# A fused chunk attention and two-layer network: the first layer in seven products for blocks 5 to 18, with sums in PSUM, and a new order

## The chip, the cores and the metric

The kernel runs on one core of a Trainium2 chip. The metric is the device time of one execution in microseconds (us); the median of three runs before the change is 275.13 us (274.96 to 275.59).

## The reference

Attention runs inside chunks of 64 tokens, for 8 batches of 576 tokens and 8 heads of 64 columns; its output, as 4608 rows of 512 columns, goes through two matrices with a leaky ReLU between them.

```python
scores = scale * np.matmul(q_c, k_c.transpose(0, 1, 2, 4, 3))   # chunks of 64 x 64
scores = scores - np.max(scores, axis=-1, keepdims=True)
attn = np.exp(scores)
attn = attn / (np.sum(attn, axis=-1, keepdims=True) + 1e-09)
out = np.matmul(attn, v_c)
...
x = np.ascontiguousarray(attn_out.transpose(0, 2, 1, 3)).reshape(B * S, H * D)
h = x @ w_in                     # 4608 x 512 by 512 x 2048
g = np.maximum(0.01 * h, h)
return (g @ w_out)               # 2048 x 512
```

## The kernel before

The tokens are worked through in 36 groups `u` of 128 rows (two chunks of all heads) for the attention, and in 19 blocks `j` for the two layers: two blocks of 128 rows, then seventeen of 256. The order of all instructions is written out by hand in one string, `ORDER`; each word is a step with its numbers, and every engine works through its own instructions strictly in the order in which the words stand.

The steps of the attention for a group are: `g` loads q and k (DMA from POOL's queue), `tq`/`tk` transpose them on PE and `q`/`k` copy them (groups 0 to 13), or `tdq`/`tdk` transpose them by a DMA from SP's queue and `cq` copies q (later groups); `s` scores (PE), `m` their maximum and `b` the subtraction (DVE), `x` the exponential (ACT), `z` sum and reciprocal (DVE), `n` the product with it (DVE, from group 10 on POOL); `e` and `c` transpose the result on PE for the first groups, `d` by DMA for the others; `v` multiplies with V (PE) and `a` copies the result to `xT` (ACT), the input of the first layer. `i` are idle products of PE that only read a constant tile; `iN` is N units of 128 columns, issued three at a time. `y` and `w` clear tiles.

The first layer of blocks 0 to 8 is plain: steps `M` (in blocks 0 to 2 partly named `A`) of 16 products of 128 columns or 8 of 256 columns each (line 319), eight per block of 256 rows, and one activation `G` (line 333, leaky ReLU from PSUM to `gT`) for each. For blocks 9 to 18 it is computed with seven products of half size in place of eight (Strassen's scheme in Winograd's form): `WS` builds four differences of w_in once, `xs` four sums of x per block (POOL or DVE, line 387), `V j.s.n` is product n for half s of the hidden columns, eight matmuls of 128 columns (line 416). Products 1, 6, 7 and 4 pile up in one bank of PSUM; after 1, 6 and 7 `lx` copies the running sum to SBUF (ACT, line 447). Products 2, 5 and 3 have other banks, and `la` adds them to those copies (DVE, line 453). `lp`, and `lx` after product 4, apply the leaky ReLU (line 435).

The second layer uses the same scheme for blocks 2 to 18: `W` builds four differences of w_out, `sum` four sums of `gT` (line 203), `R j.n` is product n, eight matmuls of 256 columns (line 227), `comb` copies (ACT, line 260) or adds (DVE, lines 264 and 281) the results and issues the store from SP's queue. Blocks 0 and 1 use plain products `B` (line 462). The last product, `R18.4`, is cut in two halves so that the first half's add and store run beside the second (line 244).

PSUM has eight banks. Before the change four of them have fixed users (`qp`, `kp`, `Sp`, `ox`) which some of the products share, and four go by the string `BANKS`.

Of the kernel before, what the change touches and what calls it, by code (L numbers as in the profile page):

```python
# [16 lines left out]
def kernel(  # L17
# [36 lines left out]

# [3 lines left out]


# [5 lines left out]
    xT = sbp.tile([128, NT, RING], FP16, name="xT")  # L65
    qk: dict[int, tuple[bass.AP, bass.AP]] = {}

    made: set[tuple] = set()

    def need(*what):  # L70
        assert what in made, what

    def load_qk(u):

        both = []
        for name, src in (("q_in", q), ("k_in", k)):
# [18 lines left out]
    def load_v_heads(b, m, h0, h1):  # L95
        if b >= NVB:
            need("batch", b - NVB)
        nc.gpsimd.dma_start(  # L98
            out=VB[b % NVB][m * CH:(m + 1) * CH, h0:h1, :, m * CH:(m + 1) * CH].rearrange("p h c d -> p (h c) d"),
            in_=v[b, m * H // 2 + h0:m * H // 2 + h1].rearrange("h (c j) d -> j (h c) d", j=CH),  # L100
        )

    def load_v(b):
        for m in range(2):
            load_v_heads(b, m, 0, H // 2)

    def load_w_in(f0, f1):
        for m in range(2):
            nc.gpsimd.dma_start(
                out=w_inT[m * CH:(m + 1) * CH, :, f0:f1],  # L110
                in_=moe_w_in[m * d_model // 2:(m + 1) * d_model // 2, f0:f1].rearrange("(t d) f -> d t f", d=D),
            )
# [51 lines left out]
    SG: dict[tuple[int, int], bass.AP] = {}
    bank: dict[tuple[int, str], bass.AP] = {}
    kept: dict[tuple[int, str], bass.AP] = {}
    opened: set[tuple[int, str]] = set()

    def weight_sum(n):
        b11, b12 = w_outT[:, :HF, :HM], w_outT[:, :HF, HM:]  # L170
        b21, b22 = w_outT[:, HF:, :HM], w_outT[:, HF:, HM:]
        x, y = {1: (b12, b11), 2: (b22, TW.get(1)), 3: (b22, b12), 4: (b21, TW.get(2))}[n]
        TW[n] = sbp.tile([128, HF, HM], FP16, name=f"TW{n}")
        nc.vector.tensor_tensor(out=TW[n], in0=x, in1=y, op=ALU.subtract)

    def rows(j):

        nh = BLOCKS[j] // 2
        halves_of = slice(0, nh), slice(nh, 2 * nh)
        return halves_of[::-1] if j in EARLY else halves_of  # L180

    def token_sums(j, n):
        if (j, n) in SG:
            return
        if j in EARLY:
            for a, p in {
                1: [(a, 1) for a in range(4)], 2: [(0, 2), (1, 2)], 3: [(0, 1), (1, 1), (0, 2), (1, 2)], 4: [(2, 2), (3, 2)],
            }[n]:
                need("act", j, a, p)
        if n in (2, 4):  # L190
            token_sums(j, n // 2)
        nh = BLOCKS[j] // 2
        one, two = rows(j)
        a11, a12 = gT[j][:, :HF, one], gT[j][:, HF:, one]
        a21, a22 = gT[j][:, :HF, two], gT[j][:, HF:, two]
        SG[j, n] = sbp.tile([128, HF, nh], FP16, name="SG", tag="gS", bufs=4, padded_shape=[128, HF, 128])
        x, y, op = {
            1: (a21, a22, ALU.add),
            2: (SG.get((j, 1)), a11, ALU.subtract),
            3: (a11, a21, ALU.subtract),  # L200
            4: (a12, SG.get((j, 2)), ALU.subtract),
        }[n]
        (nc.gpsimd if (j, n) in SG_POOL else nc.vector).tensor_tensor(out=SG[j, n], in0=x, in1=y, op=op)  # L203

    def product(j, n, i):
        one, two = rows(j)
        g, w = gT[j], w_outT
        where, left, right = {
            1: ("X", g[:, :HF, one], w[:, :HF, :HM]),
            2: ("W", g[:, HF:, one], w[:, HF:, :HM]),  # L210
            3: ("Z", SG.get((j, 4)), w[:, HF:, HM:]),
            4: ("X", g[:, HF:, two], TW.get(4)),
            5: ("Z", SG.get((j, 1)), TW.get(1)),
            6: ("X", SG.get((j, 2)), TW.get(2)),
            7: ("X", SG.get((j, 3)), TW.get(3)),
        }[n]
        if where != "X" and j in ONE:
            where = n
        if (j, where) not in bank:
            tag = None if j in EARLY else {"X": "qp", "Z": None if j in ZMM else "kp"}.get(where)  # L220
            bank[j, where] = psp.tile([128, 2, HM], FP32, name=f"pr{where}", tag=tag or mm(), bufs=1)
        to = bank[j, where]
        if j == LAST and n == 4:
            last_product(left, right)
            return
        for f in range(HF):
            nc.tensor.matmul(  # L227
                out=to[:, i, :],
                lhsT=left[:, f, i * 128:(i + 1) * 128],
                rhs=right[:, f, :],  # L230
                start=(j, where) not in opened,
# [119 lines left out]
    def w_in_sum(n):  # L351
        if len(WS) >= n:
            return
# [519 lines left out]
```

## Time and profile before

| | |
|---|---|
| time, median of three runs | 275.13 us |
| span of the profiled execution (its time beside the span isn't given) | 273.3 us |
| busy PE / DVE / ACT / POOL | 265.9 / 219.9 / 208.8 / 165.3 us |
| products of the plain first layer, line 319 | 768 |
| products of the first layer in seven, line 416 | 1120 |
| products of the second layer in seven, line 227 | 944 |
| granted clock of PE | 1.00 |

The span runs from the first to the last instruction. A row of a timeline gives start and length in us, engine, line, operation, the tile written and the tiles read. A group of products ends in the records some time after its last product could be followed by another, so the spacing of two starts is shorter than a group's length; the chain of waits shows the spacing.

### The profile page before, as it was taken

What the parts mean: (1) busy time and instruction counts of PE and PEld (TensorE: products, weight loads), DVE (VectorE), ACT (ScalarE), POOL (GpSimd) and SP (SyncE); (2) the same over time, 40 slices, a digit from 0 to 9 for tenths busy, and PEclk for the clock granted to TensorE, in tenths of its full rate; (3) what the DMA queues carried; (4) which work ended last, traced back from release to release, by engine and by line L of the source; (5) the groups of instructions that cost most, each with busy time, mean ns of one, the idle gap of its engine ahead of it and who ended that gap; (6) DMA issues with size and microseconds to landing.
All of it is one profiled execution on the core that took longest, in us unless ns stands there. A gap on an engine that the chain in (4) does not pass through costs nothing.

```text
span 273.3 us, 9009 instructions
## 1 busy us (share of the span) xinstructions
PE 265.9 (97%) x3705; PEld 242.4 (89%) x3705; DVE 219.9 (80%) x427; ACT 208.8 (76%) x410; POOL 165.3 (60%) x190
## 2 busy tenths in 40 slices
PE   7889999999999999999999999999999999999994
PEld 3579958999999899998989999999999998999994
DVE  7786869999997668798677987977899879488783
ACT  6667635665779688666999989899999998857560
POOL 8848546783175448649689799689895636012100
PEclk9999999999999999999999999999999999999999
DMA  9999999999999999999999999799999503131113
GB/s 147 155 188 191 206 178 156 176 117 130 210 138 169 171 140 119 195 219 168 164 189 153 203 160 124 139 134 180 95 147 158 134 2 101 22 98 40 41 41 115
DMA packets 159241, 38.34 MB, mean 140 GB/s; under 512 B 150240, under 2 KB 154720, under 8 KB 159200
## 3 DMA queue, kind: packets, MB, share of 16 engines
q0 software_dynamic: 111392, 18.10, 98.3%
q1 hardware_dynamic: 46768, 19.41, 38.7%
q8 instruction: 29, 0.48, 0.7%
q10 hardware_dynamic: 1040, 0.26, 0.4%
q14 instruction: 12, 0.10, 0.2%
HBM read 36.70 MB, written 9.44 MB: 169 GB/s over the span
## 4 chain that ended last, share of the span: by engine, by line
PE 86%; DVE 5%; ACT 3%; POOL 3%; issue 2%; POOLq 0%; DVEq 0%; ACTq 0%
PE hT L319 20%; PE prX L227 20%; PE xbank L416 11%; PE xpr L416 9%; PE prZ L227 6%; PE pr L227 6%; PE prW L227 3%; PE Sp L584 3%; PE xp L656 3%; PE oP L462 3%; ACT QZ L539 1%; ACT gT L435 1%; PE kp L512 1%; PE qp L512 1%; POOL SG L203 1%
## 5 line engine op out<-in xcount | busy, mean ns | idle before, releaser
L319 PE MATMUL hT<-xT,w_inT 128*128 128x128 f16 (+1 forms) x768 | 62.4, 237 | 0.0
L319 PEld LDWEIGHTS <-w_inT 128*128 128x128 f16 x768 | 53.6, 98 | 2.8
L227 PEld LDWEIGHTS <-SG 128*128 128x128 f16 x544 | 51.0, 98 | 5.4
L620 POOL TENSOR_TENSOR en<-ex,zi 128x512 f16<-128x512 f16 x26 | 28.2, 1085 | 40.1 <-DVE zi L614 19.8
L453 DVE TENSOR_TENSOR xkeep<-xpr,xkeep 128x512 f32<-128x512 f32 x60 | 39.6, 681 | 13.7 <-ACT xkeep L447 9.6
L333 ACT ACTIVATE gT<-hT 128x512 f16<-128x512 f32 x64 | 36.6, 595 | 9.0 <-PE hT L319 8.9
L227 PEld LDWEIGHTS <-gT 128*128 128x128 f16 x400 | 37.3, 98 | 4.3 <-ACT gT L435 0.4
L447 ACT ACTIVATE xkeep<-xbank 128x512 f32<-128x512 f32 x60 | 34.6, 593 | 7.4 <-PE xbank L416 7.0
L416 PEld LDWEIGHTS <-WS 128*128 128x128 f16 x640 | 38.0, 98 | 0.5
L91 POOL DMA_DIRECT2D q_in<-in_q_dram x39 | 33.4, 861 | 7.0 <-DMA w_outT<-in_moe_w_out_dram 3.0
L91 POOL DMA_DIRECT2D k_in<-in_k_dram x39 | 32.6, 838 | 7.8 <-DMA VB<-in_v_dram 3.3
L227 PE MATMUL prX<-TW,SG 128*128 128x256 f16 x272 | 35.3, 273 | 0.0
L435 ACT ACTIVATE gT<-xkeep 128x512 f16<-128x512 f32 x56 | 33.4, 631 | 2.1 <-DVE xkeep L453 1.8
L260 ACT ACTIVATE keep<-prX 128x256 f32<-128x256 f32 x51 | 19.6, 384 | 16.9 <-PE prX L227 16.5
L416 PEld LDWEIGHTS <-w_inT 128*128 128x128 f16 x480 | 29.0, 98 | 0.9 <-issue 0.4
L203 DVE TENSOR_TENSOR SG<-gT 128x1024 f16<-128x1024 f16 x34 | 25.2, 740 | 4.7 <-ACT gT L333 2.9
L610 DVE TENSOR_REDUCE z<-ex 128x8 f32<-128x512 f16 x36 | 24.4, 679 | 4.9 <-ACT ex L604 4.7
L593 DVE TENSOR_REDUCE mx<-Sp 128x8 f32<-128x512 f32 x36 | 24.4, 677 | 4.5 <-PE Sp L584 4.5
L573 ACT ACTIVATE QZ<-QT 64x512 f16<-64x512 f16 x44 | 27.3, 627 | 0.9 <-PE Sp L584 0.3
L677 ACT ACTIVATE xT<-xp 128x512 f16<-128x512 f32 x36 | 21.5, 596 | 6.0 <-PE xp L656 5.8
L387 POOL TENSOR_TENSOR xs<-xT 128x256 f16<-128x256 f16 x18 | 12.5, 701 | 20.7 <-ACT xT L677 20.7
L98 POOL DMA_DIRECT2D VB<-in_v_dram x24 | 23.4, 987 | 0.0
(92 smaller groups left out, 486.0 us busy)
## 6 DMA issues: line engine op xcount, KB each, us to landing
out_dram<-osb SPq DMA_DIRECT2D x35, 256.0 KB, 4.1
q_in<-in_q_dram POOLq DMA_DIRECT2D x31, 128.0 KB, 5.9
k_in<-in_k_dram POOLq DMA_DIRECT2D x31, 128.0 KB, 6.7
VB<-in_v_dram POOLq DMA_DIRECT2D x8, 288.0 KB, 9.1
VB<-in_v_dram POOLq DMA_DIRECT2D x16, 144.0 KB, 5.3
w_inT<-in_moe_w_in_dram POOLq DMA_DIRECT2D x8, 256.0 KB, 7.2
w_outT<-in_moe_w_out_dram POOLq DMA_DIRECT2D x4, 512.0 KB, 11.6
q_in<-in_q_dram POOLq DMA_DIRECT2D x8, 64.0 KB, 6.3
```

What stands on the lines that cost most here:

```text
L91: nc.gpsimd.dma_start(out=to, in_=rows)
L203: (nc.gpsimd if (j, n) in SG_POOL else nc.vector).tensor_tensor(out=SG[j, n], in0=x, in1=y, op=op)
L227: nc.tensor.matmul(out=to[:, i, :], lhsT=left[:, f, i * 128:(i + 1) * 128], rhs=right[:, f, :], start=(j, where) not in opened, stop=(f == ...
L319: nc.tensor.matmul(out=hT[:, i, :], lhsT=w_inT[:, t, fc * 128:(fc + 1) * 128], rhs=xT[:, t, r0:r0 + tb], start=(t == 0), stop=(t == NT - 1),)
L333: nc.scalar.activation(out=gT[j][:, nf * a:nf * a + nf, c0:c0 + tb], in_=HT.pop((j, a, p)), func=AFT.Prelu, bias=0.0, scale=1.0, alpha=0.01,)
L416: nc.tensor.matmul(out=to[:, i, :], lhsT=left[:, t, i * 128:(i + 1) * 128], rhs=right[:, t], start=(n in (1, 2, 5) and t == 0 and i == 0), ...
L435: nc.scalar.activation(out=gT[j][:, f0:f0 + 4, hi * 128:hi * 128 + 128], in_=of, func=AFT.Prelu, bias=0.0, scale=1.0, alpha=0.01)
L447: nc.scalar.activation(out=XK[j, s, n], in_=XB[j, s], func=AFT.Copy, bias=0.0, scale=1.0)
L453: nc.vector.tensor_tensor(out=to, in0=of, in1=to, op=ALU.add)
L573: nc.scalar.activation(out=to, in_=QT[u][part], func=AFT.Copy, bias=0.0, scale=1.0)
L593: nc.vector.tensor_reduce(out=MX[u], in_=SP[u], axis=AXL.X, op=ALU.max)
L620: (nc.gpsimd if u >= UP else nc.vector).tensor_tensor(out=E[u], in0=ex, in1=ZI.pop(u).unsqueeze(2).to_broadcast((128, 8, CH)), op=ALU.mult)
```

## The change

The first layer of blocks 5 to 8 goes over to seven products; blocks 0 to 4 stay plain. In all fourteen blocks with seven products the sums are formed in another way: after product 1 a copy `ls` puts it in a second bank of PSUM (`seed`), on which product 2 is accumulated; product 5 is copied to SBUF (`lf`); `la` adds that copy to the sum of products 1 and 6, back into the bank of product 5, on which product 3 is then accumulated, and to the sum of products 1, 6 and 7; product 4 is accumulated in the first bank. Four activations `lp` read the three banks and the one tile in SBUF.

All steps stand in a new order, with `z` cut in three, `W` and `WS` in two, and the stores as steps `st` of their own. A word that ends in `'` runs on the other engine of its kind: copies on DVE in place of ACT, sums and `n` on POOL in place of DVE, the leaky ReLU on DVE, the small addition in `z` on ACT. The second string, `BANKS`, now names the bank of each of PSUM's tiles and the buffer of each tile in SBUF; some tiles get more buffers (`KT` 4 for 3, `ex` 4 for 2, `en` 4 for 3, `et` 5 for 4, sums of `gT` 5 for 4).

```diff
...
+    def copy(other, to, of):
+        if other:
+            nc.vector.tensor_copy(out=to, in_=of)
         else:
+            nc.scalar.activation(out=to, in_=of, func=AFT.Copy, bias=0.0, scale=1.0)
...
+    def leaky(other, to, of):
+        if other:
+            nc.vector.scalar_tensor_tensor(out=to, in0=of, scalar=0.01, in1=of, op0=ALU.mult, op1=ALU.max)
+        else:
+            nc.scalar.activation(out=to, in_=of, func=AFT.Prelu, bias=0.0, scale=1.0, alpha=0.01)
...
+    def wide(j, s, n):
...
+        if n == 1:
+            XB[j, s] = ps([128, 4, 128], "xbank")
+        elif n == 5:
+            XZ[j, s] = ps([128, 4, 128], "xz")
+        to = {2: XW, 3: XZ, 5: XZ}.get(n, XB)[j, s]
+        for i in range(4):
+            for t in range(2):
+                nc.tensor.matmul(
+                    out=to[:, i, :],
+                    lhsT=left[:, t, i * 128:(i + 1) * 128],
+                    rhs=right[:, t],
+                    start=(n in (1, 5) and t == 0 and i == 0),
+                    stop=(t == 1),
+                    skip_group_check=True,
+                )
+
+    def wide_seed(j, s, other=0):
+        XW[j, s] = ps([128, 4, 128], "seed")
+        copy(other, XW[j, s], XB[j, s])
+
+    def wide_five(j, s, other=0):
+        X5[j, s] = sb([128, 4, 128], FP32, "x5", "xkeep", 6)
+        copy(other, X5[j, s], XZ[j, s])
+
+    def wide_add(j, s, n):
+        to = XZ[j, s] if n == 3 else X5[j, s]
+        nc.vector.tensor_tensor(out=to, in0=XB[j, s], in1=X5[j, s], op=ALU.add)
+
+    def wide_leaky(j, s, n, other=0):
+        second, hi = {2: (0, 0), 4: (0, 1), 3: (1, 0), 5: (1, 1)}[n]
+        of = {2: XW, 4: XB, 3: XZ, 5: X5}[n][j, s]
+        f0 = 8 * s + 4 * second
+        leaky(other, hidden(j)[:, f0:f0 + 4, hi * 128:hi * 128 + 128], of)
...
     ORDER = (
-        "i33 y4 y2 I y0 y6 y1 tq0 q0.0 q0.1 w3 tk0 i5 k0 i6 s0 tq1 i4 m0 b0 q1.1.1 i13 tk1 q1.0.1 x0 k1 tq2 i8 s1 tk2 "
-        "z0 m1 b1 k2.1 n0 i6 q2.0.1 q2.1.1 x1 i9 i7 i13 e0 c0.1 z1 s2 tk3 v0 tq3 m2 n1 b2 a0 e1 c1 i7 v1 A0.0 x2 a1 "
...
+        "g1 i11.2 i73.0 g2 y4 y5 y1 y0 I If y3' y2' g3 tq0 i2.1 tk0 tq1 k0' tk1 q0.1' q0.0 s0 m0 L0 q1.1 k1 q1.0 tq2 tk2 "
+        "b0 x0 k2 q2.1 s1 q2.0' g4 m1 z0.0 Q0 z0.1' tq3 i8.7 i28.4 b1 x1 z0.2 n0' s2 m2 Q1 tk3 k3 i7.6 z1.0 z1.1' q3.0 "
+        "i42.5 b2 z1.2 n1' q3.1' x2 s3 e0 i6.3 z2.0 z2.1' z2.2 n2' c0 v0 e1 a0 tq4 e2 m3 b3 x3 c1' c2' z3.0 g5 v1 tk4 v2 "
+        "a2 M0.0.0 M2.0.1 k4 G2.0.1 z3.1 z3.2 a1' M1.0.0 q4.0' n3 M2.1.1 e3 q4.1' s4 m4 G1.0.0 c3 M0.1.0 Q2 v3 a3 b4 x4 "
...
-        "comb18.6 R18.3.0 comb18.0 comb18.3 comb17.3 R18.7.0 comb18.7 R18.2.0 comb18.5 comb18.2 R18.4.0 comb18.4 "
+        "comb18.0 comb18.3 R17.4 comb18.2 comb17.4 st17.1 sum18.3' st18.0 R18.7 comb18.7 R18.4 comb18.5 st18.1.1 "
```

More of the change, by code (lines that the diff above doesn't have):

```diff
@@ L176, in rows @@
[L176 to L183, printed above, removed]
-            return
[L185 to L231, printed above, removed]
-                stop=(f == HF - 1),
-                skip_group_check=True,
-            )
-            opened.add((j, where))
@@ L735, with stage_a, hidden, part_of @@
-    ORDER = (
[84 rows of a table removed]
+    def stage_a(u, other=0):
+        at = u * G % RING
+        copy(other, xT[:, :, at:at + G], XP[u])
+        groups.add(u)
+    gT: dict[int, bass.AP] = {}
+    HT: dict[tuple[int, int, int], bass.AP] = {}
+    def hidden(j):
+        if j not in gT:
+            gT[j] = sb([128, NFC, BLOCKS[j]], FP16, "gT", "gT", 3, padded_shape=[128, NFC, NB])
+        return gT[j]
+    def part_of(j, p):
+        return (128, (p - 1) * 128) if p else (BLOCKS[j], 0)
+    def mm1(j, a, p=0):
+        tb, c0 = part_of(j, p)
+        rows_ready(START[j] + c0, START[j] + c0 + tb)
+        r0 = (START[j] + c0) % RING
+        nf = 512 // tb
+        hT = ps([128, nf, tb], "hT")
+        for i in range(nf):
+            fc = nf * a + i
+            for t in range(NT):
+                nc.tensor.matmul(
+                    out=hT[:, i, :],
+                    lhsT=w_inT[:, t, fc * 128:(fc + 1) * 128],
+                    rhs=xT[:, t, r0:r0 + tb],
+                    start=(i == 0 and t == 0),
+                    stop=(t == NT - 1),
+                    skip_group_check=True,
+                )
+        HT[j, a, p] = hT
@@ new lines, in product @@
+    def product(j, n):
+        one, two = halves_of(j)
+        g, w = gT[j], w_outT
+        where, left, right = {
+            1: ("X", g[:, :HF, one], w[:, :HF, :HM]),
+            2: ("W", g[:, HF:, one], w[:, HF:, :HM]),
+            3: ("Z", SG.get((j, 4)), w[:, HF:, HM:]),
+            4: ("X", g[:, HF:, two], TW.get(4)),
+            5: ("Z", SG.get((j, 1)), TW.get(1)),
+            6: ("X", SG.get((j, 2)), TW.get(2)),
+            7: ("X", SG.get((j, 3)), TW.get(3)),
+        }[n]
+        if where == "Z" and j in FIVE:
+            where = f"Z{n}"
+        if n in (1, 2, 5) or where == "Z3":
+            bank[j, where] = ps([128, HM], f"pr{where[0]}")
+        to = bank[j, where]
+        if j == LAST and n == 4:
+            last_product(left, right)
+            return
+        for f in range(HF):
+            nc.tensor.matmul(
+                out=to,
+                lhsT=left[:, f, :],
+                rhs=right[:, f, :],
+                start=(f == 0 and (n in (1, 2, 5) or where == "Z3")),
+                stop=(f == HF - 1),
+                skip_group_check=True,
+            )
@@ new lines, in mm2, with plain_out, store @@
+    def mm2(j, ti, part):
+        if part == 0:
+            oP[j, ti] = ps([128, d_model], "oP")
+        for fc in range(part * 4, part * 4 + 4):
+            nc.tensor.matmul(
+                out=oP[j, ti],
+                lhsT=gT[j][:, fc, ti * 128:(ti + 1) * 128],
+                rhs=w_outT[:, fc, :],
+                start=(fc == 0),
+                stop=(fc == NFC - 1),
+            )
+    def plain_out(j, ti, other=0):
+        copy(other, output(j, ti), oP[j, ti])
+    def store(j, t, c=2):
+        r0 = START[j] + (t * 128 if j in PLAIN else halves_of(j)[t].start)
+        cut = slice(0, d_model) if c == 2 else slice(c * HM, c * HM + HM)
+        nc.sync.dma_start(out=out[r0:r0 + 128, cut], in_=ob[j, t][:, cut])
```

666 lines of the change are left out of this document (239 added, 427 removed), and 165 rows, old and new, of the table ORDER.

## The prediction

> **What bounds the kernel now.** First the page: the span and the busy times. Then the busy times by stretch, the chain of waits for the price of each product, and the timeline of the start.
>
> ```profile
> span 273.3 us, 9009 instructions
> ...
> PE 265.9 (97%) x3705; PEld 242.4 (89%) x3705; DVE 219.9 (80%) x427; ACT 208.8 (76%) x410; POOL 165.3 (60%) x190
> ```
>
> Columns of the next view: stretch, its length, then busy time and instruction count of PE, PEld, DVE, ACT, POOL, the granted clock, the DMA share and GB/s (the first two lines are of PE alone).
>
> ```profile
> 17.41:269.76 252.35, 251.87 (x3516) 1.00 1.38 139
> 269.76:273.30 3.54, 0.00 (x1) 1.00 0.45 148
> ```
>
> ```profile
> 40.00:80.00 40.00, 40.00 (x595) 37.26 (x594) 37.72 (x78) 25.31 (x52) 23.84 (x28) 1.00 2.23 155
> ```
>
> From the first real product of the first layer to the last product, PE stands idle for half a microsecond in 252. So three things set the end: when PE becomes full, how much work it has from there, and the 3.5 us after its last product. The third row shows that DVE can run at 37.72 of 40 us (94%) without costing PE anything. The chain of waits gives the spacing of products when nothing holds them (start, us, what):
>
> ```profile
> 22.23 0.22 PE qp L512 x4
> ...
> 27.37 0.23 PE Sp L584 x8
> ...
> 83.57 2.62 PE hT L319 x24
> ...
> 257.45 0.89 PE xbank L416 x16
> ...
> 265.38 0.87 PE prX L227 x8
> ```
>
> A step of eight products costs 0.873 us when 256 columns wide (2.62 / 3, and 0.87 in the second layer), 0.446 us when 128 wide (0.89 / 2).
>
> **The products of blocks 5 to 8.** Per block 8 steps `M` of 256 columns (6.98 us) become 14 steps `V` of 128 columns (6.24 us): 0.74 us saved, 2.95 us for four blocks. Blocks 9 to 18 already have 14 such steps, and the second layer keeps its seven. All of it lies on PE, so it would come off the span whole if PE stayed as full.
>
> **The start.** Here the new order adds to PE's list. The idle fillers `i` go from 111 units of 128 columns to 177, and 84 of them now stand ahead of `tq0`, where 33 stood. Timeline of PE in the first 22 us (start, us):
>
> ```profile
> 1.33 3.50 PE L686 MATMUL idle<-warm 128*128 128x384 f16 x11 [1.33 <-DVE zeros L137]
> 4.71 0.63 PE L512 MATMUL qp<-ident,q_f 128*128 128x128 f32 x4
> 5.46 0.66 PE L512 MATMUL kp<-ident,k_f 128*128 128x128 f32 x4
> 5.95 0.76 PE L686 MATMUL idle<-warm 128*128 128x384 f16 x4
> ...
> 7.77 0.44 PE L517 MATMUL qp<-ident,q_in 64*64 64x64 f16 x16
> ...
> 17.44 1.95 PE L319 MATMUL hT<-xT,w_inT 128*128 128x128 f16 x32
> ...
> 20.05 1.06 PE L319 MATMUL hT<-xT,w_inT 128*128 128x128 f16 x16
> ...
> 21.17 1.06 PE L319 MATMUL hT<-xT,w_inT 128*128 128x128 f16 x16
> 22.07 0.39 PE L512 MATMUL qp<-ident,q_in 128*128 128x128 f16 x4
> ```
>
> Eleven fillers of three units took 3.50 us, 0.32 us each; by 5.95 the same filler takes about 0.16 us (0.76 for 11 units, less the 0.17 us by which a group's last end lies past its spacing). So the first 33 units run until 4.8 as now, and the 51 added ones take 51 x 0.054 = 2.8 us more: `tq0` starts at 7.6 instead of 4.71 (at 8.1 if the fast rate comes as late as 5.95). The durations for what follows are these groups (x count | busy, mean ns):
>
> ```profile
> L453 DVE TENSOR_TENSOR xkeep<-xpr,xkeep 128x512 f32<-128x512 f32 x60 | 39.6, 681 | 13.7 <-ACT xkeep L447 9.6 <-PE xpr L416 3.9
> ...
> L620 POOL TENSOR_TENSOR en<-ex,zi 128x512 f16<-128x512 f16 x26 | 28.2, 1085 | 40.1 <-DVE zi L614 19.8 <-ACT xkeep L447 9.8 <-ACT gT L435 3.0
> ...
> L203 DVE TENSOR_TENSOR SG<-gT 128x1024 f16<-128x1024 f16 x34 | 25.2, 740 | 4.7 <-ACT gT L333 2.9 <-ACT gT L435 1.8
> L610 DVE TENSOR_REDUCE z<-ex 128x8 f32<-128x512 f16 x36 | 24.4, 679 | 4.9 <-ACT ex L604 4.7
> L593 DVE TENSOR_REDUCE mx<-Sp 128x8 f32<-128x512 f32 x36 | 24.4, 677 | 4.5 <-PE Sp L584 4.5
> ...
> L203 POOL TENSOR_TENSOR SG<-gT,SG 128x1024 f16<-128x1024 f16 x8 | 17.4, 2173 | 9.3 <-DVE SG L203 4.0 <-ACT keep L260 2.7 <-ACT xkeep L447 2.6
> ...
> L281 DVE TENSOR_TENSOR osb<-prZ,keep 128x256 f32<-128x256 f32 x22 | 9.3, 421 | 4.6 <-PE prZ L227 3.1 <-ACT keep L260 1.2
> ...
> L614 DVE RECIPROCAL zi<-ze 128x8 f32<-128x8 f32 x36 | 7.3, 203 | 2.7
> ...
> L598 DVE TENSOR_TENSOR sh<-Sp,mx 128x512 f32<-128x512 f32 x9 | 6.2, 685 | 0.2
> ...
> L637 DVE COPY et<-tpe 128x512 f16<-128x512 f16 x4 | 1.6, 409 | 1.5 <-PE tpe L628 1.5
> ...
> L550 DVE COPY KT<-kp 128x512 f16<-128x512 f16 x2 | 1.4, 721 | 0.0
> ...
> L541 DVE CAST QZ<-qp 64x512 f16<-64x512 f32 x2 | 1.3, 656 | 0.0
> ```
>
> The new list puts `s3`, `tq4`, `tk4`, `e2` and `v2` of PE ahead of the first `M`, so that `M0.0.0` waits for the attention of group 2. Followed through: 7.6, `tq0` 0.6, `tk0` 0.7, then on DVE `k0'` and `q0.1'` (0.66 each, one behind the other): 10.2; `s0` 0.4. From there to `z2.2` DVE has fourteen instructions in a row: three each of `m`, `b` and the reduction of `z` (0.68), two copies of group 2 and 3 (0.72), three reciprocals (0.2), 8.2 us: 18.8, some 19.2 with the small additions `z1.1'` and `z2.1'`, now on ACT, between them. `n2'` on POOL 1.05: 20.3; transposition, `c2'` and the issue of `v2` 1.0: `M0.0.0` at 21.3. In the run shown, PE would have reached the same point of its work at 18.95: it is at 22.07 with four steps of 0.89 of `hT` done (rows of x32, x16, x16) and without two transpositions of 0.22. The start loses 2.3 us. The bounds: if no wait is left, PE's own list (7.6, then 93 units of filler, 5.0, and the transpositions, scores and values, 6.5) ends at 19.1, a loss of 0.2; with the later clock and every wait a little longer 22.5, a loss of 3.5. I take 2.3, the sum that the rows give.
>
> POOL's list changes too: group 4's loads now stand ahead of the quarters of w_in, and `n0'` to `n2'` between the loads.
>
> ```profile
> 17.59 0.61 POOL L109 DMA_DIRECT2D w_inT<-in_moe_w_in_dram  x1 [0.65 <-DMA w_inT<-in_moe_w_in_dram]
> ...
> 26.32 0.90 POOL L91 DMA_DIRECT2D q_in<-in_q_dram  x1 [0.80 <-DMA w_inT<-in_moe_w_in_dram]
> ...
> 31.69 0.89 POOL L91 DMA_DIRECT2D q_in<-in_q_dram  x1 [1.29 <-DMA w_outT<-in_moe_w_out_dram]
> ```
>
> The first quarter of w_in is in at 17.6 today; between 26.3 and 31.7 the queue passes, among others, one group's q and k and a quarter of w_out, of which the group can have at most half. So the quarter lands between 17.6 and 20.3, ahead of 21.3: nothing. If `n2'` is late, group 5's loads behind it are late, and `tk5` has seven steps `M` of cover.
>
> **DVE and the other engines.** Per half block the first layer now takes two adds (`la`), a seed copy (`ls`), a copy (`lf`) and four activations, eight operations where blocks 9 to 18 had ten. In blocks 5 to 8 they replace four. Beside this the new order moves thirty copies of `comb` (priced as the add, 0.42), ten of `a`, thirteen of `ls` and `lf` to DVE, and eleven sums more to POOL. In the order from `V5.1.1` to `R10.6` PE has 96 `V`, 41 `R` and 28 products of scores and values: 85.1 us. DVE has 26 `la`, 14 each of `m`, `b` and `z`, 20 sums, 32 `comb`, 22 small steps of `z`, 13 `xs` and 21 others: 95 us at the durations above. Independent ones follow each other faster than they last:
>
> ```profile
> 41.55 0.68 DVE L620 TENSOR_TENSOR en<-ex,zi 128x512 f16<-128x512 f16 x1
> 42.14 0.69 DVE L203 TENSOR_TENSOR SG<-gT,SG 128x1024 f16<-128x1024 f16 x1
> ```
>
> That is 0.59 for 0.68, so the 95 us need some 83: DVE is nearly as full as PE. The bounds: nothing, since 83 fits into 85; or 83 / 0.943 = 88, if DVE can't be driven past the 94% of the row above, 3 us, and 5 us with what follows below on POOL. I take 1.5, nearer the row in which PE lost nothing, because the steps ahead of and behind this stretch are lighter and an add can slip into them.
>
> ACT, busy 208.8 us, loses the 32 activations of blocks 5 to 8, 60 copies and the forty that went to DVE, and gets some 90 operations in their place, 18 of them small: it gets emptier, nothing. The `ls` copies write PSUM, which no row shows on ACT; between 0.4 and 0.7 they stay hidden.
>
> Sums on POOL last 2.17 us against 0.74 on DVE, nineteen of them instead of eight. One event shows what they can do to DVE:
>
> ```profile
> 204.40 1.98 DVE L203 TENSOR_TENSOR SG<-gT 128x1024 f16<-128x1024 f16 x1
> ...
> 204.76 1.06 POOL L620 TENSOR_TENSOR en<-ex,zi 128x512 f16<-128x512 f16 x1
> ```
>
> A sum that usually starts 0.6 us after its predecessor and lasts 0.7 took 1.98 us beside an operation of POOL. [...]
>
> **The end.** `comb18.5` and its store now follow `R18.4`, so that DVE adds one more piece (0.42) after the last one, and a store of that half row leaves last: 0.4 us. Bounds 0 and 0.8. The other stores become steps of their own on SP, later than their last add; the transposes behind them wait no longer than now: nothing.
>
> Sum: 273.3 - 2.95 + 2.3 + 1.5 + 0.4 = 274.55 us of span. The page gives no time beside the span; the median of the runs, 275.13, lies 1.83 above it, so 276.4.
>
> **The rivals.** First, *the saved columns show* (faster): the fillers only fill what would be idle, waits at the start vanish, DVE fits. 273.3 - 2.95 + 0.2 + 0 + 0.4 = 270.95, time 272.8. For it speaks that PE keeps 0.2% idle beside a DVE at 94%; against it that 66 units of filler, 3.6 us, are more than the columns saved, in a queue that works in order. Second, *the start takes just what the products give*: 2.3 to 2.8 and 0.4 against 2.95, no wait at DVE: 275.0 to 275.4. Third, *DVE becomes the bound* of blocks 5 to 10: 5 us there and 1 us of shutting out: 279.05 and 1.83, 280.9; it decides once adds are late by more than PE's work at hand, and 83 of 85 us speaks for it, the lighter neighbours against it.
>
> **The numbers.** Forecast 0.40, first rival 0.29, second 0.18, third 0.13. Under 0.2% (0.55 us) is what a measurement of this kernel can't tell from no change: the second is "same", the first "faster", the others "slower", 0.53. The range 272.5 to 281.0 takes in the first and third and leaves out some 0.14; the forecast's own is 275.7 to 278.5.
>
> **What would show it.** The start: `hT` of block 0 first at 21 us, a filler block until 7.6. The products: 196 steps of 0.446 in the first layer's line. DVE: a share above 95% between 75 and 165 us, and waits of PE on DVE there. The end: an add behind the last product's. It is wrong if `hT` starts before 19.5, or if PE loses under 0.5 us or over 4 us after it.

## The result and the profile after

The changed kernel takes 289.49 us (median of four runs, 288.28 to 290.77) against 275.36 us of the kernel before beside it (274.96 to 275.85): a ratio of 1.051, 95% interval 1.047 to 1.055. It is slower, by 14 us. The prediction had said slower, 276.4 us, and a range up to 281.0. The runs of the new order spread more than those of the old one; each profile below is of one execution, whose own time lies some 1.8 us above its span (289.2 us for the span of 287.4). A ratio is worked out from the fast executions of both kernels, those within 1.5% of the fastest, while a median is over all of them.

First the page of the kernel after: span, busy times, PE and its clock in 40 slices.

```profile
span 287.4 us, 9457 instructions
...
PE 272.3 (95%) x3918; PEld 248.6 (87%) x3918; DVE 230.1 (80%) x470; ACT 190.0 (66%) x370; POOL 183.4 (64%) x198
...
PE   8699999999999999999799779999999999999994
...
PEclk9969999999999999999989979999999999999999
```

In the row of PE there are two dents behind the start, in slices 20 and 23 to 24 (a slice is 7.2 us), and the clock is below full at those places and in the third slice of the start. Busy times by stretch, cut at these places (columns as in the prediction: stretch, length, PE, PEld, DVE, ACT, POOL, granted clock, DMA share, GB/s):

```profile
0.00:25.89 25.89, 21.31 (x243) 13.69 (x244) 14.89 (x30) 12.39 (x21) 16.94 (x27) 0.87 1.34 125
25.89:138.88 112.99, 112.31 (x1714) 104.22 (x1711) 100.64 (x214) 86.36 (x169) 79.81 (x91) 1.00 1.88 164
138.88:147.00 8.12, 6.25 (x82) 5.67 (x80) 4.82 (x10) 3.39 (x6) 1.33 (x2) 0.79 2.13 189
...
162.72:171.30 8.58, 4.86 (x56) 4.22 (x54) 7.43 (x11) 4.16 (x8) 7.08 (x7) 0.80 1.49 136
171.30:283.16 111.86, 111.86 (x1600) 105.82 (x1597) 87.05 (x180) 71.50 (x144) 66.37 (x59) 1.00 0.68 98
283.16:287.40 4.24, 0.00 (x0) 0.00 (x0) 0.62 (x2) 0.00 (x0) 0.00 (x0) 0.84 0.44 148
...
100.00:120.00 20.00, 20.00 (x305) 19.01 (x303) 19.65 (x42) 17.41 (x38) 14.54 (x17) 1.00 1.69 185
```

So PE is as full as before over 240 us, and the loss stands in four places. The start: the first `hT` comes at 25.89 where the kernel before stood at the same point of PE's work at 18.95, 6.9 us. Two holes in the middle, with a low granted clock behind them (0.79 and 0.80 in their stretches). And the end, 4.24 us for 3.54. The last line belongs to the dispute on DVE: busy 19.65 of 20 us (98%), and PE loses nothing.

**The start.** Timeline of PE, then of DVE:

```profile
1.33 7.07 PE L194 MATMUL idle<-warm 128*128 128x384 f16 x29 [1.33 <-DVE zeros L163]
8.23 0.61 PE L222 MATMUL qp<-ident,q_f 128*128 128x128 f32 x4
...
11.58 0.41 PE L277 MATMUL Sp<-KT,QZ 128*128 128x64 f16 x8 [1.58 <-ACT QZ L200]
...
13.66 0.61 PE L277 MATMUL Sp<-KT,QZ 128*128 128x64 f16 x8 [1.05 <-ACT QZ L200]
...
14.76 4.02 PE L194 MATMUL idle<-warm 128*128 128x384 f16 x13
...
19.71 2.84 PE L194 MATMUL idle<-warm 128*128 128x384 f16 x17
...
25.89 1.28 PE L370 MATMUL hT<-xT,w_inT 128*128 128x128 f16 x20
```

```profile
12.03 0.69 DVE L284 TENSOR_REDUCE mx<-Sp 128x8 f32<-128x512 f32 x1 [1.19 <-PE Sp L277]
...
15.54 0.72 DVE L198 COPY QZ<-qp 64x512 f16<-64x512 f16 x1 [2.09 <-ACT QZ L200]
...
19.25 0.69 DVE L284 TENSOR_REDUCE mx<-Sp 128x8 f32<-128x512 f32 x1 [1.12 <-PE Sp L277]
...
23.16 0.20 DVE L305 RECIPROCAL z<-z 128x8 f32<-128x8 f32 x1 [0.28 <-ACT z L301]
```

The prediction's chain can be laid beside it: `tq0` at 8.23 for 7.6 (0.6 late); `s0` 3.35 behind it for 2.6, since the second half of the copy to `QZ` is on ACT and starts when DVE's half is done (0.75); from the first maximum at 12.03 to the end of the last reciprocal at 23.36 it is 11.3 us for 8.2 to 8.6, because DVE is not "fourteen instructions in a row": it waits 2.09 us for a copy on ACT and 1.12 for a score (2.7 in all); the rest 2.5 for 2.1 (0.4). Together some 4.5 of the 4.6 us by which 25.89 lies behind 21.3. One of these waits is PE's own doing: 13 fillers take 4.02 us, 0.31 us each, while a few us later 17 take 2.84, 0.17 each. After holes of 1.58 and 1.05 us PE ran at half its rate (granted clock 0.52 from 14 to 20 us), and the score behind the 13 fillers came 1.9 us late.

**The holes.** Timeline of PE around 139 and around 163 us:

```profile
138.88 0.61 PE L442 MATMUL xz<-xs,WS 128*128 128x128 f16 x8
141.36 0.69 PE L335 MATMUL xp<-et,VB 128*128 128x64 f16 x16 [1.87 <-DMA k_in<-in_k_dram]
...
142.34 1.61 PE L442 MATMUL xbank<-xs,WS 128*128 128x128 f16 x16
...
144.60 1.76 PE L525 MATMUL prX<-TW,SG 128*128 128x256 f16 x8
146.20 0.61 PE L442 MATMUL xbank<-xs,WS 128*128 128x128 f16 x8
```

```profile
162.84 0.40 PE L277 MATMUL Sp<-KT,QZ 128*128 128x64 f16 x8
166.95 1.86 PE L525 MATMUL prX<-TW,SG 128*128 128x256 f16 x8 [3.72 <-DVE keep L198]
168.61 1.71 PE L442 MATMUL xbank<-xT,w_inT 128*128 128x128 f16 x16
...
171.05 1.04 PE L525 MATMUL prX<-TW,gT 128*128 128x256 f16 x8
```

At 139 `v18` and `v19` wait for the transposition of `en` by DMA (`d18`, `d19`): `d18` goes out at 132.29 and lands 8.9 us later, at 141.2; the row names a load that landed last. From 138.88 to 146.20 lie 7.32 us with work for 3.57 (0.45, 0.47, 0.45, 0.89, 0.45, 0.87): 3.75 lost, 1.87 by waiting and the rest because products of 0.87 us take 1.60 behind the hole (granted clock 0.50 from 143 to 146). At 163, 8.21 us from 162.84 to 171.05 hold work for 2.88: 5.33 lost, 3.72 by waiting for a copy `keep` on DVE, the rest at a low clock. What DVE did in that time, the group to which the instruction belongs (x count | busy, mean ns), and POOL beside it:

```profile
160.04 5.32 DVE L309 TENSOR_TENSOR en<-ex,z 128x512 f16<-128x512 f16 x1
```

```profile
L309 DVE TENSOR_TENSOR en<-ex,z 128x512 f16<-128x512 f16 x13 | 13.5, 1041 | 0.1
```

```profile
160.72 1.12 POOL L309 TENSOR_TENSOR en<-ex,z 128x512 f16<-128x512 f16 x1
161.72 1.35 POOL L418 TENSOR_TENSOR xs<-xT 128x256 f16<-128x256 f16 x2
162.96 0.95 POOL L117 DMA_DIRECT2D q_in<-in_q_dram  x1
163.90 0.90 POOL L117 DMA_DIRECT2D k_in<-in_k_dram  x1
164.80 2.54 POOL L502 TENSOR_TENSOR SG<-gT 128x1024 f16<-128x1024 f16 x1
```

`n23`, which the new order leaves on DVE, lasts 5.32 us; its twelve likes last 0.68 on average (13.5 less 5.32, over twelve). It ends at 165.36, 0.56 behind POOL's last load issue. The sum: 6.94 (start) + 3.75 + 5.33 + 0.70 (end) + 0.20 (more idle time in the first long stretch) = 16.92. The span grew by 14.1 us, so 2.8 is left for what the products save, forecast as 2.95.

### The profile page after: what moved, and what is told of

It reads as the page before. It is cut to its first block, busy times and chain, and to the rows that moved or that the text cites. A ratio compares the mean times of both kernels' runs of the same rounds, so it can differ in the third digit from the quotient of the medians.

```text
span 287.4 us, 9457 instructions
## 1 busy us (share of the span) xinstructions
PE 272.3 (95%) x3918; PEld 248.6 (87%) x3918; DVE 230.1 (80%) x470; ACT 190.0 (66%) x370; POOL 183.4 (64%) x198
## 4 chain that ended last, share of the span: by engine, by line
PE 78%; DMA 10%; POOL 4%; DVE 4%; ACT 2%; issue 1%; DVEq 0%; POOLq 0%; ACTq 0%
PE prX L525 19%; PE xbank L442 16%; PE prZ L525 9%; PE xz L442 8%; PE hT L370 5%; PE prW L525 5%; DMA w_outT<-in_moe_w_out_dram 5%; PE seed L442 4%; PE idle L194 4%; DMA k_in<-in_k_dram 3%; PE Sp L277 2%; PE xp L335 2%; DMA KT<-k_in 2%; PE oP L571 2%; DVE en L309 2%; POOL q_in L117 1%
## 5 line engine op out<-in xcount | busy, mean ns | idle before, releaser
L442 PEld LDWEIGHTS <-WS 128*128 128x128 f16 x896 | 55.1, 98 | 0.9
L309 POOL TENSOR_TENSOR en<-ex,z 128x512 f16<-128x512 f16 x23 | 24.2, 1054 | 30.7 <-DVE z L305 21.5
L442 PE MATMUL xbank<-xs,WS 128*128 128x128 f16 x448 | 33.6, 221 | 0.0
L370 PE MATMUL hT<-xT,w_inT 128*128 128x128 f16 x512 | 31.4, 219 | 0.0
L502 POOL TENSOR_TENSOR SG<-gT 128x1024 f16<-128x1024 f16 x10 | 21.7, 2167 | 12.9 <-PE xbank L442 7.2
L384 ACT ACTIVATE gT<-xz 128x512 f16<-128x512 f32 x28 | 16.7, 595 | 13.1 <-PE xz L442 7.7
L384 ACT ACTIVATE gT<-xbank 128x512 f16<-128x512 f32 x28 | 16.2, 592 | 9.2 <-PE xbank L442 9.0
L461 DVE TENSOR_TENSOR xz<-xbank,x 128x512 f32<-128x512 f32 x28 | 19.4, 695 | 3.5 <-PE xbank L442 1.8
L461 DVE TENSOR_TENSOR x<-xbank,x 128x512 f32<-128x512 f32 x28 | 18.9, 681 | 3.4 <-PE xbank L442 3.3
L384 ACT ACTIVATE gT<-hT 128x512 f16<-128x512 f32 x32 | 17.8, 598 | 5.6 <-PE hT L370 5.6
```

Source lines behind the costliest of these rows:

```text
L309: (nc.gpsimd if other else nc.vector).tensor_tensor(out=EN[u], in0=EX[u], in1=Z[u, 2].unsqueeze(2).to_broadcast((128, 8, CH)), op=ALU.mult)
L370: nc.tensor.matmul(out=hT[:, i, :], lhsT=w_inT[:, t, fc * 128:(fc + 1) * 128], rhs=xT[:, t, r0:r0 + tb], start=(i == 0 and t == 0), stop=( ...
L384: nc.scalar.activation(out=to, in_=of, func=AFT.Prelu, bias=0.0, scale=1.0, alpha=0.01)
L442: nc.tensor.matmul(out=to[:, i, :], lhsT=left[:, t, i * 128:(i + 1) * 128], rhs=right[:, t], start=(n in (1, 5) and t == 0 and i == 0), st ...
L461: nc.vector.tensor_tensor(out=to, in0=XB[j, s], in1=X5[j, s], op=ALU.add)
L502: (nc.gpsimd if other else nc.vector).tensor_tensor(out=SG[j, n], in0=x, in1=y, op=op)
```

## The experiments

Each starts from the changed kernel; a word that moves takes its digits of `BANKS` along. Times are medians, with the ratio to the kernel before on the same chip.

### Fewer fillers in front

```diff
-"g1 i11.2 i73.0 g2 ...
+"g1 i11.2 i22.0 g2 ...
```

> The changed kernel with 33 units of filler ahead of the first transposition in place of 84, nothing else. Theory A (the filler in front delays the whole start, 2.8 us of it): the first transposition starts near 5.3 us in place of 8.2, the first-layer product near 23, time 289.5 - 2.9 = 286.6 us. Rival B (the start waits for something else, data or the granted clock, and the filler only fills): first-layer product still near 25.9, time 289.5.

Measured: 285.63 us, ratio 1.036 (1.029 to 1.042). `tq0` starts at 5.15, the first `hT` at 23.60, 2.3 us earlier:

```profile
12.47 4.02 PE L194 MATMUL idle<-warm 128*128 128x384 f16 x13
...
23.60 1.11 PE L370 MATMUL hT<-xT,w_inT 128*128 128x128 f16 x17
```

The slow fillers stay (4.02 us again). The 51 added units cost what they delay `tq0` by (3.1 us), less a little, as theory A has it. Beyond the start this execution gains at the hole of 139, which nothing in the edit touches: 1.9 us are lost there (137.75 to 143.22) instead of 3.75.

### The holes of the start filled

```diff
-... tk1 q0.1' ... tk2 b0 ...
+... tk1 i28 q0.1' ... tk2 i16 b0 ...
```

> The changed kernel with the 84 units in front kept and 44 more units of filler put where PE stood idle between 10 and 14 us (28 behind the transposition of k of group 1, 16 behind that of k of group 2). Theory A (in the changed kernel PE ran at half rate from 14 to 19.7 us since it had stood idle before, 13 fillers in 4.02 us): all fillers run at 0.16 us per three units, the first-layer product starts near 23.9, time 287.4 us. Rival B (the chain over DVE and ACT sets the start, the rate of PE doesn't matter): first-layer product at 25.9 or later, time 289.5 to 290.

Measured: 287.0 us, ratio 1.040 (1.036 to 1.044). The first stretch, and the timeline of PE:

```profile
0.00:23.70 23.70, 20.32 (x257) 13.28 (x258) 14.79 (x30) 12.35 (x21) 16.94 (x27) 1.00 1.42 137
```

```profile
13.39 2.13 PE L194 MATMUL idle<-warm 128*128 128x384 f16 x13
...
23.74 0.94 PE L370 MATMUL hT<-xT,w_inT 128*128 128x128 f16 x14
```

44 units more, and the first `hT` comes 2.15 us earlier: the clock is 1.00 for 0.87, and the same 13 fillers take 2.13 us for 4.02. But 1.0 of this lies ahead of the holes: in this execution the 29 fillers in front take 6.08 us for 7.07, and `tq0` starts at 7.25 for 8.23. From `tq0` to the first `hT` it is 16.5 us for 17.7, so the filled holes are worth 1.2 us. The 1.9 us saved on the 13 fillers do not come through whole, since a later score then waits 1.20 us for a copy on DVE: both theories have a part.

### n23 on POOL

```diff
-... sum9.3 n23 n22' tdq28 ...
+... sum9.3 n23' n22' tdq28 ...
```

> The changed kernel with one instruction moved: the normalisation of group 23 on POOL in place of DVE, where it lasted 5.32 us beside operations of POOL. Theory A (that one instruction was shut out and held DVE and PE): no wait of PE near 163 us, no slow products behind it, time 289.5 - 5.3 = 284.2 us. Rival B (DVE has too much work in blocks 5 to 10 and falls behind anyway): the wait moves some us later, time 288 or more.

Measured: 281.94 us, ratio 1.025 (1.020 to 1.030); 7.5 us gained, of the span 7.3: 5.3 is the hole, 0.7 an earlier start in this execution (first `hT` at 25.18), and 2.0 the hole at 139, which is smaller here though the edit does not touch it (a wait of 1.52 us with no slow products behind it, 1.8 lost for 3.75); a new wait of 0.56 at 107.7 takes some of that back. The stretch from 157 to 177, in this run and in the changed kernel:

```profile
157.00:177.00 20.00, 19.97 (x309) 18.94 (x307) 18.14 (x34) 15.85 (x32) 19.76 (x22) 1.00 1.70 175
```

```profile
157.00:177.00 20.00, 16.28 (x219) 14.98 (x217) 18.10 (x29) 12.51 (x25) 14.43 (x17) 0.91 1.30 143
```

The hole is gone, with POOL now busy 19.76 of 20 us and DVE 18.14. One instruction on another engine is worth 5 us: `n23` was held on DVE, and DVE's load was not the cause of the hole.

### d18 earlier

```diff
-... R8.1 vl4.1 g25 ... a16 n18' V9.0.1 ... xs9.4 d18 v18 v19 ...
+... R8.1 n18' vl4.1 d18 g25 ... a16 V9.0.1 ... xs9.4 v18 v19 ...
```

> The changed kernel with the normalisation of group 18 ahead of the loads of V and of group 25 on POOL, and the transposition by DMA of group 18 right behind it in the order, ahead of a store and of the transpositions of groups 19 and 24 on SP. Theory A (the product with V of group 18 waited near 139 us for that transposition, which took 9 us behind loads): no wait of PE near 139 us, time 289.5 - 3.7 = 285.8 us. Rival B (the DMA engines are so full there that another transposition is late instead): the wait moves to the next product with V, time 288.5 or more.

Measured: 290.2 us, ratio 1.054 (1.049 to 1.059): no gain. `v18` is in time (138.65), and now `v19` waits to the same moment:

```profile
141.51 0.41 PE L335 MATMUL xp<-et,VB 128*128 128x64 f16 x8 [2.46 <-DMA et<-en]
```

It is not the place of one issue: now `d19` goes out late, at 133.16, takes 8.3 us and lands at 141.4. That is the outcome that theory B expects.

The size of this hole isn't steady. In the five runs that leave these transpositions, their consumers and all loads ahead of them in place, the wait of `v18` and `v19` is 0.44 us (holes filled), 1.52 (n23 on POOL), 1.57 (fewer fillers), 1.95 (x sums moved) and 2.80 (load issues moved), for 1.87 in the changed kernel. A single execution can't price a cure at this place.

### The two loads in front of d18 and d19 issued later

```diff
-... g29 st6.0 ... sum7.4 g26 cq22.0 tdq24 d19 ... d18 v18 v19 V9.0.5 ...
+... st6.0 ... sum7.4 cq22.0 tdq24 d19 ... d18 v18 v19 g29 g26 V9.0.5 ...
```

> The loads of groups 29 and 26 are issued behind v19 instead of ahead of d19 and d18; nothing else differs from the changed kernel. Theory A, the transposing transfers of n18 and n19 land late (up to 9.4 us) because these loads of four times 512 KB fill the transfer engines: they land within 6 us, the stall of 1.9 us at 139 and the 1.8 us of half-rate products behind it go, time 285.8 to 287. Theory B, the transposing transfers are late because of what stands on their own queue or because n18 itself comes late: the stall stays above 1.5 us and the time within 0.7 us of 289.5.

Measured: 288.29 us (284.13 to 288.9), ratio 1.039 (1.031 to 1.047). Both products with V run at 141.97 without a wait, and a later one waits instead:

```profile
163.15 0.39 PE L335 MATMUL xp<-et,VB 128*128 128x64 f16 x8 [3.84 <-DMA et<-en]
```

`d18` and `d19` land after 6.4 and 6.2 us, for 8.9 and 9.4. This fits theory A, but doesn't show it: with the loads in place they land after 6.6 to 9.6 us in six executions, and in the first run of all cures below, with the same move, after 7.2 and 7.7. (By the page each of these loads is 128 KB, not 512.) The later wait has a cause that can be read: `d21` itself lands after an ordinary 4.9 us, but goes out at 158.12, 5.5 us later than in the changed kernel, because the transposition of keys ahead of it in SP's queue (`tdk28`, at 156.84) waits 4.6 us for k of group 28, whose load stands behind the moved ones, and `d21` follows it. This execution took 288.81 us and the fastest of the four 284.13, so the 3.84 us need not be in every one.

### What holds n23: POOL's two x sums moved, then the load issues moved

```diff
-... a21 xs11.3' xs11.1' cq25.1 ... m25 sum10.3' st7.0 ...
+... a21 cq25.1 ... m25 sum10.3' xs11.3' xs11.1' st7.0 ...
```

> The two products x - of block 11 that stand on GpSimd between n22 and the loads of group 33 (1.35 us) go behind the sum SG of block 10; n23 stays on VectorE. GpSimd then runs n22 (160.7 to 161.8), two load issues (to 163.6), SG. Theory A, VectorE's addition of two SBUF inputs is held from GpSimd's first arithmetic until the issues are over too: n23 takes 4.1 us (5.32 before), the stall at 163 shrinks by 1.1 us, time 288.4. Theory B, only GpSimd's arithmetic holds it: n23 takes 2.3 us, the stall goes from 3.9 to about 1 us and most of the slow products behind it go too, time 285.5. Theory C, it is held until GpSimd's whole list there is done: n23 takes over 6 us, time 290.4.

Measured: 285.17 us, ratio 1.035 (1.032 to 1.039). `n23` of this run, and POOL's `n22` with what follows:

```profile
158.97 2.35 DVE L309 TENSOR_TENSOR en<-ex,z 128x512 f16<-128x512 f16 x1
```

```profile
159.65 1.11 POOL L309 TENSOR_TENSOR en<-ex,z 128x512 f16<-128x512 f16 x1
161.07 0.95 POOL L117 DMA_DIRECT2D q_in<-in_q_dram  x1 [0.32 <-ACT QZ L200]
```

2.35 us, as theory B has it: `n23` ends 0.56 us behind POOL's arithmetic, and the load issues that follow after a pause of 0.32 us do not hold it. The moved x sums come late in their turn: PE waits 1.54 us for them at 166.80. The other half:

```diff
-... b24 g33 s25 m25 sum10.3' st7.0 ...
+... b24 s25 m25 sum10.3' g33 st7.0 ...
```

> Changed kernel with the loads of group 33 issued behind SG of block 10, so that GpSimd runs n22, two x -, and SG without a load issue between them; n23 stays on VectorE. In the changed kernel n23 took 5.32 us and ended 0.56 us behind the end of the load issues; with the two x - moved away it took 2.35 and ended 0.56 us behind n22, ahead of the issues. Theory A, the issues alone hold nothing and what holds n23 is arithmetic only: it ends 0.56 us behind the last x -, 3.6 us. Theory B, the issues held it when they follow the x - without a gap: n23 is let in at the next boundary of GpSimd's arithmetic, here between n22 and x - or between x - and SG, 2.3 to 3.6 us. Theory C, GpSimd's SG directly behind keeps it out as well: over 5.5 us. Time 286.5 to 288 by A and B, 290 by C.

Measured: 290.16 us, ratio 1.050 (1.042 to 1.058).

```profile
160.19 5.67 DVE L309 TENSOR_TENSOR en<-ex,z 128x512 f16<-128x512 f16 x1
```

```profile
160.88 1.11 POOL L309 TENSOR_TENSOR en<-ex,z 128x512 f16<-128x512 f16 x1
...
163.14 2.16 POOL L502 TENSOR_TENSOR SG<-gT 128x1024 f16<-128x1024 f16 x1
```

Theory C: without issues in between, the sum SG holds it too, and `n23` ends 0.56 us behind that (165.30). So DVE's instruction was not let in at three boundaries of POOL's instructions that follow without a pause: four in a row held it for 4.4 us. This is no rule for every boundary. In the run before (x sums moved), a sum on DVE, usually 0.69 us long, ends 0.55 us behind POOL's sum SG (162.91 to 165.05), although two x sums follow that one without a pause:

```profile
163.96 1.64 DVE L502 TENSOR_TENSOR SG<-gT,SG 128x1024 f16<-128x1024 f16 x1
```

```profile
164.99 1.76 POOL L418 TENSOR_TENSOR xs<-xT 128x256 f16<-128x256 f16 x2
```

In the changed kernel `n23` got in behind two load issues that followed the x sums without a pause (it ends at 165.36, 0.56 us behind the second, 164.80). Two other traces point to the issues themselves: with n23 on POOL, a sum on DVE ends at 162.88, 0.57 us behind the first of two load issues that follow x sums (162.31), and in the second form of all cures at 160.04, 0.58 behind (159.46). What decides at which boundary DVE is let in stays open.

### The four cures together, in two forms

```diff
-... i73.0 ...  ... tk1 q0.1' ...  ... tk2 b0 ...  ... n23 n22' ...  ... R18.4 comb18.5 st18.1.1
+... i22.0 ...  ... tk1 i28 q0.1' ...  ... tk2 i16 b0 ...  ... n23' n22' ...  ... comb18.5 st18.1.1 R18.4
```

with the loads later as above:

> Together: 33 filler units ahead of the first transposition, 44 filler units in the two holes behind it, n23 on GpSimd, the loads of groups 29 and 26 behind v19, and the last block's sixth sum with its store ahead of the last product. If the four causes are independent: span 287.4 - 5.5 (start) - 5.3 (n23) - 3.5 (transposing transfers) - 0.6 (tail) = 272.5, time 274.3; if the loads are not the cause of the late transfers 277.8. What would be left of a rival that the products of 128 columns cost more elsewhere: a time above 279.

or with the loads in place and the products with V later:

```diff
-... d18 v18 v19 V9.0.5 ... g28 a19 xs10.1' V9.1.6 ... V9.1.2 lp9.1.2 ...
+... d18 V9.0.5 ... g28 V9.1.6 ... V9.1.2 v18 v19 a19 xs10.1' lp9.1.2 ...
```

> As the run with all together, but the loads of groups 29 and 26 stay where they are and v18, v19 (with what follows from v19) go four products later in TensorE's list, so that 1.8 us of products cover the wait for the transposing transfers. Span 272.5 to 273.5, time 274.3 to 275.3 if what follows v19 is not itself late; if VectorE's sums of block 10 are then late, a stall of 1 to 2 us appears behind them and the time is 276 to 277.

Measured: 281.07 us, ratio 1.018 (1.014 to 1.023) with the loads later, where `v18` and `v19` still wait 0.70 us and the same later product with V 2.29; 278.88 us, ratio 1.015 (1.010 to 1.019) with `v18` and `v19` later, the best form that was found, and still slower than the kernel before. Its stretches:

```profile
0.00:22.68 22.68, 19.16 (x241) 12.49 (x242) 14.84 (x30) 12.35 (x21) 16.95 (x27) 1.00 1.54 143
22.68:272.52 249.84, 248.43 (x3682) 232.63 (x3678) 211.83 (x439) 177.30 (x349) 167.29 (x173) 1.00 1.44 138
```

PE loses 1.4 us in 250 and the clock is full throughout. What is left against the kernel before: 3.7 us of start, 0.9 at the end (4.48 us behind PE's last product for 3.54; the moved store gained nothing: the last stores now queue on SP one behind the other, five from 271.20 to 274.10), and 0.9 more idle time. Against that, PE's busy time behind the start is 1.9 us shorter (248.43 against 251.87 - 1.54), where the products should give 2.95. About 0.6 of the other 1.0 is idle time as well, which the records hide, since a group's last end lies 0.17 us past its spacing: by the spacing of the starts, the waits behind the start take some 2.7 us, and some 1.2 in the kernel before. The rest was not traced.

### What is left of the start

Two runs on top of the last form. In the first, group 0's way to the first layer goes ahead of the other groups':

```diff
-... x0 k2 q2.1 s1 q2.0' g4 m1 z0.0 Q0 z0.1' ... s3 e0 ... c0 v0 e1 a0 ... a2 M0.0.0
+... x0 z0.0 Q0 z0.1' k2 q2.1 z0.2 n0' s1 q2.0' g4 m1 ... e0 c0 ... v0 a0 ... M0.0.0 e1 s3 ... a2
```

> As the run with v18 and v19 later, and in the start the first group's way to the first layer goes ahead of the later groups: the sum over its exponentials ahead of the third group's copies, its normalisation and transposition ahead of the fourth group's scores, the first quarter of w_in issued ahead of group 4's loads, M0.0.0 right behind a0; 49 filler units fewer and 14 more. Theory A, what is left of the start's cost (first M at 22.68, where an undelayed M0.0.0 of the kernel before would stand at 18.95) is that the new order takes the first group's rows through the queues behind the other groups: M0.0.0 starts at 18 to 19.5, span 273.5 to 275, time 275.3 to 276.8. Theory B, the start is bound by loads (w_in, q and k) and M0.0.0 may come early but what stands behind it waits: span above 276, time above 277.8.

Measured: 281.66 us (279.64 to 285.88), ratio 1.018 (1.010 to 1.025). In the profiled execution, at 285.88 us the slowest of five, `M0.0.0` stands at 20.20, but the next `M` only at 25.08, with PE waiting in between for copies on DVE (1.03 us) and ACT (0.69). Moving one group forward moves the others back, as theory B has it; that loads are the reason isn't seen in these waits.

In the second, the whole start (groups 0 to 5, blocks 0 to 2, fillers, engines, loads) has the order of the kernel before, and the new order follows. The last block's last add also goes back behind `R18.4`, its place in the changed kernel:

```diff
-"g1 i11.2 i73.0 g2 y4 y5 ... tq0 i2.1 tk0 tq1 k0' tk1 q0.1' q0.0 s0 ... a2 M0.0.0 ... G2.2.2 ...
+"g1 I g2 g3 L0 Q0 Q1 g4 Q2 Q3 g5 i33 y4 y2 If ... tq0 q0.0' q0.1' y3' tk0 i5 k0 i6 s0 ... a0 e1 c1' i7 v1 M0.0.0 ... G2.2.2
```

> The order of the kernel before up to the last act of block 2's first layer (groups 0 to 5, its fillers, its engines, its loads up to group 5), then the new order for all that is left, with n23 on GpSimd and v18, v19 four products later. Theory A: what remains of the start's cost in the run with v18 and v19 later (first M at 22.68 instead of 18.95 or earlier) is the new order of the start alone: M0.0.0 stands at 17.4 to 18, and 277.0 - 3.5 = 273.5 of span, 275.3 of time, level with the kernel before. Theory B: the new order behind the start is behind in its other work too (groups 6 to 8, whose loads and transpositions stand on the same queues): holes of 1 us and more open between 25 and 110, time above 277.

Measured: 280.19 us (278.51 to 284.54), ratio 1.013 (1.009 to 1.018).

```profile
18.56 3.33 PE L370 MATMUL hT<-xT,w_inT 128*128 128x128 f16 x32 [1.07 <-DMA w_inT<-in_moe_w_in_dram]
...
39.86 0.59 PE L222 MATMUL qp<-ident,q_in 128*128 128x128 f16 x4 [2.71 <-ACT gT L384]
...
143.99 0.69 PE L335 MATMUL xp<-et,VB 128*128 128x64 f16 x16 [2.63 <-DMA et<-en]
```

The first `hT` stands at 18.56, but its order of steps is that of the kernel before, so it has to be counted like that one's 18.95: PE reaches the point that was at 22.07 there at 24.44 here, which makes 21.3. That is 1.4 us earlier than in the form above and still 2.4 later than in the kernel before: the first `hT` waits 1.07 us for a quarter of w_in, and it and the score behind it run slowly (32 products in 3.33 us for 1.95, the score's eight in 0.64 for 0.40; the mean granted clock of this execution is 0.98, that of the form above 1.00). So the new order of the start is part of its remaining cost, and the clock and the loads are another. The gain is given back: PE waits 2.71 us at 39.86 for a copy on ACT and 1.04 at 108.59 for transposed keys, and the products with V at 144, four places later in the list as in that form, wait 2.63 us for a transposition once more. This execution took 284.54 us, the slowest of five, so its holes need not be those of the others; the median shows no gain over the last form. Theory B comes nearer: holes of over 1 us opened between 25 and 110, and one behind.

## Why the prediction was wrong

**Direction and size.** Slower was right, with the chance of 0.53; 289.5 lies 13 us above the forecast and 8.5 above the range. The direction had a sound reason, since the start alone (6.9 us) costs more than the products save; but 9.1 us come from two holes in the middle that the sum put at nothing or hid in another term. Term by term:

**The products.** The count is right: 1568 products in the first layer's new line, 196 steps, at the spacing of 0.446. Of the 2.95 us the changed kernel shows 2.8, by what the other terms leave, and the last form 1.9.

**The start, 2.3 us in a range of 0.2 to 3.5: measured 6.9.** The step that failed is the chain "fourteen instructions in a row" on DVE. It priced the instructions of one engine and not the places where this engine waits for ACT and PE, 2.09 and 1.12 us in the rows above. And it took the fillers behind the first ones at the fast rate; that PE slows down again in the holes of the start, worth 1.2 us by the run with the holes filled, was in no term. No single hole in front of the slow fillers is longer than 1.6 us in this trace; they lie close together (PE busy 1.38 of the 4 us from 10 to 14), and behind them the granted clock was 0.52 (14 to 20 us).

**DVE's load, 1.5 us, and the third rival: nothing.** DVE was driven to 98% from 100 to 120 us without a loss of PE, so the bound of 88 us for blocks 5 to 10 was too careful. The rival's 280.9 came nearer to the result than the forecast, but by luck: DVE as the bound, 5 us of it, is not seen, and its 1 us of shutting out became 5.3. No run shows that 1 us, nor the 2 us for POOL by which the bound above the 1.5 rose from 3 to 5; what the runs showed in its place is the one event that follows.

**POOL shutting DVE out: one event of 5.3 us instead of a share in 1.5.** The prediction had the right row, a sum of 1.98 us beside an operation of POOL, and the wrong unit: an instruction against an instruction. What was measured is one instruction on DVE held over several of POOL's, 5.32 and 5.67 us. And it took what DVE loses as load, to be spread, where it is a delay of one chain: the copy `keep` stands behind `n23` in DVE's order, and PE's next product waits 3.72 us for the bank that this copy frees. How the one holds the other isn't shown. The rows give only when: `n23`'s record begins 0.7 us ahead of that of POOL's `n22` (160.04 and 160.72, in the run of four 160.19 and 160.88) and ends 0.56 us behind a later one of POOL's instructions (164.80, in the run of four 165.30).

**The transposing DMAs, "nothing": 3.75 us.** This is the step that said that the transposes behind the stores "wait no longer than now": it looked at the stores on SP alone. `d18` goes out at 132.3, 7 us before `v18` could start, and lands after 8.9 us; the longest of all these transpositions in the kernel before took 7.3. Why it lands late is open in part. The loads of groups 26 and 29 stand close ahead in the new order, and the run with them later fits, but the wait changes between 0.44 and 2.80 us in runs that move none of this. What the runs do show is that the new order leaves a distance between `d18`, `d19` and their consumers that is too short in every execution that has them unchanged, by 0.4 to 2.8 us.

**The end, 0.4 in 0 to 0.8: 0.7.** The mechanism was right in kind (the add ends 0.3 us later behind PE's last product, the rest is the last store's issue, which waits on SP behind two others and goes out at 284.39), and moving the add alone did not cure it.

**What no term held.** The two holes of PE cost their own length and then products at half the rate: 3.75 for 1.87, 5.33 for 3.72. This price is no fixed factor, and the length of the hole alone doesn't set it: holes of 1.57 us (fewer fillers, 138) and 2.46 (d18 earlier, 139) left the granted clock at 1.00 (130 to 150 us), and behind one of 2.27 (group 0 first, 13) five fillers took 0.92 us, the full rate, while behind the one of 1.07 at 18 us in the last run 32 products took 3.33 us for 1.95. What decides was not found.

The first rival (272.8) fell at its first step, the start; the second, that the start takes just what the products give, with it.

## What to carry to other kernels

In an order written out by hand, walk the chain of a start through all engines, with a wait at each change of engine: the sum of one engine's instructions, here 8.2 us where 11.3 were measured, is a lower bound only. Where GpSimd and VectorE both combine tiles from SBUF, look at what stands directly behind GpSimd's instruction: here one of VectorE's lasted 5.67 us over a run of four without a pause and 2.35 over one instruction, and the cure was to put that one on the other engine (some 5 us). Where a product waits for a transposition by DMA, ask what its queue waits for before shifting loads: here a shifted load held up the queue by 4.6 us and with it the next transposition, for which PE waited 3.84, and moving the consumer later helped in one form and not in the next. And price a hole from several executions: the wait of the one at 139 changed sixfold, from 0.44 to 2.80 us, without an edit near it.

## What the runs showed of the hardware

A fall of the granted clock behind short holes: 128x384 products of the changed kernel took 0.16 us each from 6.2 to 8.2 us (granted clock 1.00) and 0.31 us from 14.8 (0.52 from 14 to 20), with holes of at most 1.6 us in between; with the same holes filled they stayed at 0.16. And the reverse: a single hole of 2.46 us with the clock at 1.00 from 130 to 150 us around it, and one of 2.27 behind which five such products took 0.92 us, the full rate.

An operation of VectorE on two inputs in SBUF, 0.68 us on average in its twelve other cases of the changed kernel, lasted 2.35 us beside one instruction of GpSimd and 5.67 us beside four that follow without a pause, and ended each time 0.56 us after the last of those. In the prediction's row the sum on VectorE ends the same 0.56 us behind GpSimd's instruction (206.38 and 205.82). A sum of 1.64 us in another trace (x sums moved) ended at 165.60, 0.55 us behind the first (165.05) of two instructions that follow without a pause.
